# Local attention scores on both row halves of the array, two PSUM banks for them, and attention work at fixed slots

## The chip, the core and the metric

One core of a Trainium2 chip runs the whole program. Its engines are PE (TensorE, the matrix multiplier), DVE (VectorE), ACT (ScalarE) and POOL (GpSimd); SP issues the DMA transfers. Matmul results land in PSUM, which has eight banks of 512 fp32 per partition; DVE and ACT read PSUM, POOL does not. The metric is device time in microseconds (us), lower is better. Three runs of the kernel before took 862.6 to 864.3 us, median 864.2.

## What is computed

```python
scores = scale * np.matmul(q, k.transpose(0, 1, 3, 2))     # B=8, H=8, S=576, D=64
mask_local = (rel >= 0) & (rel < stride)                   # heads 0..3, stride 32
mask_strided = (rel >= 0) & (pos[None, :] % stride == pos[:, None] % stride)   # heads 4..7
attn = softmax(np.where(mask, scores, -1e9))
x = (attn @ v) as (4608, 512)                              # tokens by heads*dims
h = x @ w_in                                               # 512 -> 2048
out = (h * cos(h)) @ w_out                                 # 2048 -> 512
```

All data are fp32, and fp32-like precision is kept by splitting operands into a high and a low part.

## The kernel before

**Two stages.** The first stage (up to about 480 us) computes attention and `h`; the second (line L705) multiplies `h*cos(h)` with `w_out`. The change touches the first stage only.

**Slots.** In the first stage the hidden products of batch b are issued on PE in 56 slots per batch (`PER_BATCH`): about one product in each slot, six matmuls of 128x128 by 288 columns (L499 for batch 0, L528 later). Products write the banks `m` (three buffers), `n` and `o`. The attention of batch b+1 is put between the products of batch b, so that it is ready when batch b+1 begins. `in_turn` fixes PE's order to the order of the code; the other engines' order is made by a scheduler that lists instructions by their estimated readiness.

**Attention units.** A batch has four strided units and three local units. A unit is: loads of `qk` and `v`; scores on PE into a PSUM bank; softmax (DVE adds the mask, takes the maximum, subtracts, all from PSUM; ACT takes exp; DVE sums, adds an epsilon and inverts; POOL multiplies, line L284); a transpose (strided: PE, L383, then ACT copies to `pt`, L387; local: DVE, L322); products with `v` on PE (strided L396, local L331); copies out of PSUM (strided: ACT, L404 and L410; local: ACT L350 and DVE L351).

A fp32 matmul counts as two passes in the profile. A local unit has 24 score matmuls of a 64-row by 32-column tile of the array, 64 columns streamed (L314); its four heads use four of the eight such tiles: column quarter c, row half c mod 2. A strided unit has 10 or 12 score matmuls on two of the four 64x64 tiles (L366); a strided product uses the other two (L396). A burst is what is issued in one go: the products of an earlier unit with the scores of a new one. In strided bursts the two are interleaved matmul by matmul, in local bursts the products stand first and the scores behind.

**Where bursts stand.** Bursts are spread evenly by interpolation (`KNOTS`), 5.2 slots apart up to slot 48, then 8. A strided unit's transposes come 3 slots after the next burst; its products come in the burst of the strided unit after the next, so that two strided units are under way. A local unit is multiplied in the next local burst.

**PSUM banks of attention in these slots.** Scores of both kinds: `acc0` (zeroed once by one wide matmul, L262, and then always written with the flag that starts an accumulation). Strided transposes, and the local products of heads 2 and 3: `acc1`. Strided products, and the local products of heads 0 and 1: `acc2`. So a bank that scores leave late delays only the next scores, and a late copy out of `acc2` delays only the next products.

**Around the start of batch 1.** Between slots 47 and 57 of each batch the seven operands of the next batch are made: DVE subtracts (L465), ACT rounds to the high part (`x_hi`, L179), POOL takes the low part (`x_lo`, L180). In batch 0 and the first slots of batch 1 POOL also has the sums and low parts of `w_in` (L180, L206 to L212).

## Time and profile before

| | us |
|---|---|
| median of three runs (lowest, highest) | 864.2 (862.6, 864.3) |
| the profiled execution | 862.53 |
| its span, first to last instruction | 860.7 |
| PE busy | 849.2 (99%) |
| second stage (L705), from 480.4 us on | 376.8 of the chain |

The granted clock is 1.00 throughout. PE is the bound: time changes where PE's own work changes, or where PE waits. The trace is to be read for two things: how long PE is held by each kind of burst, and how late DVE, ACT and POOL hand back the banks and tiles that PE waits for. The rows are in the section below the next one.

### The profile page before, as it was taken

How to read it: one execution, taken by the hardware profiler on the slowest of the kernel's cores; microseconds unless marked ns; L12 is line 12 of the kernel's file. 1: busy time of each engine (PE TensorE's matmuls, PEld its weight loads, DVE VectorE, ACT ScalarE, POOL GpSimd, SP SyncE). 2: the span in 40 equal slices, each digit the busy share in tenths (PEclk: the TensorE clock that was granted, in tenths of full speed). 3: DMA queues.
4: the chain of work that ended last, by engine and by line, in shares of the span. 5: the costliest groups of instructions: out<-in, count | busy, mean ns of one | idle time of the engine just before them, and what ended most of it. 6: DMA issues, size and time to landing. Idle time of an engine off the chain costs nothing.

```text
span 860.7 us, 23160 instructions
## 1 busy us (share of the span) xinstructions
PE 849.2 (99%) x9147; PEld 792.2 (92%) x9147; DVE 569.3 (66%) x1087; ACT 529.1 (61%) x1031; POOL 540.1 (63%) x543
## 2 busy tenths in 40 slices
PE   9899999999999999999999999999999999999998
PEld 5799999999999999999999889999999999999996
DVE  5888766758667667686433667767777676767671
ACT  3766545545444454454457787777777777777772
POOL 2578984416216144162175489889888989898961
PEclk9999999999999999999999999999999999999999
DMA  9688444565667566765466844444444444444330
GB/s 335 207 272 298 140 161 167 177 211 196 240 214 240 195 226 227 233 218 201 152 198 210 283 123 135 123 126 132 124 124 130 126 123 126 132 125 130 118 129 28
DMA packets 91902, 151.82 MB, mean 176 GB/s; under 512 B 8465, under 2 KB 53009, under 8 KB 91793
## 3 DMA queue, kind: packets, MB, share of 16 engines
q1 hardware_dynamic: 91072, 150.11, 53.2%
q8 instruction: 72, 1.18, 0.6%
q14 instruction: 38, 0.30, 0.1%
q10 hardware_dynamic: 720, 0.23, 0.1%
HBM read 96.30 MB, written 54.00 MB: 175 GB/s over the span
## 4 chain that ended last, share of the span: by engine, by line
PE 89%; POOL 3%; DMA 3%; DVE 2%; ACT 2%; issue 1%; SPq 0%; DVEq 0%; ACTq 0%; POOLq 0%
PE q L705 44%; PE m L528 19%; PE n L528 10%; PE o L528 5%; PE m L499 4%; PE acc L331 2%; PE acc L396 2%; PE acc L314 2%; POOL x_lo L180 2%; DMA h_all<-h 1%; PE acc L383 1%; PE acc L366 1%; DMA v<-in_qkl 1%; DMA v<-in_qkvs 0%; PE m L314 0%
## 5 line engine op out<-in xcount | busy, mean ns | idle before, releaser
L705 PE MATMUL q<-w,g_hi 128*128 128x512 f32 (+1 forms) x1000 | 200.3, 339 | 0.0
L705 PEld LDWEIGHTS q<-w,g_hi 128*128 128x128 f32 x1000 | 161.1, 190 | 21.2
L180 POOL TENSOR_TENSOR g_lo<-g,g_hi 128x896 fp32r<-128x896 f32 x78 | 165.6, 2137 | 7.5 <-ACT g_hi L179 6.7
L705 PE MATMUL q<-w,g_lo 128*128 128x512 f32 (+1 forms) x500 | 111.7, 339 | 0.0
L528 PE MATMUL m<-x_hi,v 128*128 128x288 f32 x448 | 110.0, 300 | 1.2 <-ACT m L536 1.2
L528 PE MATMUL m<-x_hi,w 128*128 128x288 f32 x448 | 109.2, 298 | 0.8 <-DVE h L546 0.8
L651 DVE SCALAR_TENSOR_TENSOR r<-wave,h_in 128x512 f32<-128x512 int32 x144 | 96.1, 685 | 15.4 <-ACT wave L650 13.9
L653 ACT ACTIVATE wave<-r,quarter 128x512 f32<-128x512 f32 x144 | 98.7, 690 | 6.2 <-DVE r L651 5.9
L179 ACT CAST g_hi<-g 128x896 fp32r<-128x896 f32 x78 | 73.7, 944 | 40.4 <-POOL g L674 28.0
L705 PEld LDWEIGHTS q<-w,g_lo 128*128 128x128 f32 x500 | 83.5, 190 | 10.2
L650 ACT ACTIVATE wave<-h_in 128x512 int32<-128x512 f32 x144 | 83.8, 593 | 7.7 <-DVE g_lo L180 7.5
L705 PE MATMUL q<-v,g_hi 128*128 128x256 f32 x624 | 87.6, 283 | 0.0
L705 PEld LDWEIGHTS q<-v,g_hi 128*128 128x128 f32 x624 | 80.5, 192 | 0.0
L528 PEld LDWEIGHTS m<-x_hi,v 128*128 128x128 f32 x448 | 78.0, 188 | 2.5 <-ACT m L536 1.7
L528 PEld LDWEIGHTS m<-x_hi,w 128*128 128x128 f32 x448 | 78.0, 188 | 2.0 <-DVE h L546 1.3
L284 POOL TENSOR_TENSOR pn_s<-e_sb,z 128x324 f32<-128x324 f32 x28 | 21.0, 750 | 93.2 <-DVE z L282 62.6
L180 DVE TENSOR_TENSOR g_lo<-wave,g_hi 128x512 fp32r<-128x512 f32 x54 | 37.2, 689 | 55.5 <-PE q L705 55.3
L536 ACT COPY m<-m 128x288 f32<-128x288 f32 x112 | 44.6, 398 | 45.6 <-PE m L528 39.3
L284 POOL TENSOR_TENSOR e_sb<-e_sb,z 128x384 f32<-128x384 f32 x24 | 20.3, 845 | 76.6 <-DVE z L282 72.7
L528 PE MATMUL m<-x_lo,w 128*128 128x288 f32 x224 | 66.1, 295 | 0.0
L528 PE MATMUL m<-x_lo,v 128*128 128x288 f32 x224 | 66.1, 295 | 0.0
L671 POOL TENSOR_TENSOR g<-g 128x256 f32<-128x256 f32 x78 | 57.8, 741 | 6.1
(137 smaller groups left out, 2054.5 us busy)
## 6 DMA issues: line engine op xcount, KB each, us to landing
h_all<-h SPq DMA_DIRECT2D x128, 288.0 KB, 2.8
h_in<-h_all SPq DMA_DIRECT2D x144, 256.0 KB, 2.8
qk<-in_qkvs SPq DMA_DIRECT2D x28, 324.0 KB, 4.2
out<-o SPq DMA_DIRECT2D x35, 256.0 KB, 3.1
qk<-in_qkl SPq DMA_DIRECT2D x21, 416.0 KB, 4.2
raw<-in_w_in SPq DMA_DIRECT2D x16, 512.0 KB, 5.4
raw<-in_w_out SPq DMA_DIRECT2D x16, 512.0 KB, 4.9
v<-in_vl SPq DMA_DIRECT2D x24, 224.0 KB, 3.8
```

The source lines that it names most:

```text
L179: with_product(cast(out=hi, in_=x))
L180: return rest.tensor_tensor(out=lo, in0=x, in1=hi.bitcast(F32), op=ALU.subtract)
L284: nc.gpsimd.tensor_tensor(out=pn, in0=e, in1=z[:, :n].unsqueeze(2).broadcast_to([P, n, w]), op=ALU.mult)
L314: self.scored = self.pe(nc.tensor.matmul(s_ps[quarter_of(c), t * KW:(t + 1) * KW], q_t[half(j), p, QB * t:QB * (t + 1)], k_t[half(j), p, Q ...
L499: in_turn(nc.tensor.matmul(self.banks[i, j], a[:, c * P:(c + 1) * P], y[:, c], start=k == 0 and m == 0, stop=k == 1 and m == len(ops) - 1, ...
L528: in_turn(nc.tensor.matmul(bank, a[:, c * P:(c + 1) * P], y[:, c], start=first and i == 0, stop=i == len(ops) - 1, skip_group_check=True,))
L536: nc.scalar.copy(out=t, in_=self.bank[name[0]])
L650: with_product(nc.scalar.activation(out=k, in_=h, func=AF.Copy, scale=1.0 / (2.0 * math.pi), bias=0.25))
L651: nc.vector.scalar_tensor_tensor(out=r, in0=k, scalar=-2.0 * math.pi, in1=h, op0=ALU.mult, op1=ALU.add)
L653: sin = nc.scalar.activation(out=wave, in_=r, func=AF.Sin, bias=quarter)
L671: by_gpsimd(pool.tensor_tensor(out=g[:, 5:7], in0=g[:, 0:5:4], in1=g[:, 1:2].broadcast_to([P, 2, P]), op=ALU.subtract))
L705: in_turn(nc.tensor.matmul(at, a, w, start=first, stop=True, skip_group_check=True))
```

## The change

1. **Local scores on eight tiles.** From batch 1 on, a local unit's six query blocks are split in two halves ("sides") of three. Side 1 has the row halves of its heads exchanged (host layout: `turned`, `twice`), so that the four heads of both sides fill all eight 64x32 tiles. Each side writes a PSUM bank of its own: one tile `wide` of two banks holds the scores. The 24 matmuls are the same; they are issued four of side 0, four of side 1, in turn. DVE's three operations read both banks in one instruction. The load of `qk` grows from 832 to 896 columns.
2. **Banks.** `wide` takes the places of `acc0` and `acc1`. Strided scores use its first bank. Strided transposes, strided products and the local products of heads 0 and 1 share the one bank `acc`; the local products of heads 2 and 3 go to `o`, the bank of the hidden product in slots 2, 9, 16 and so on. The scratch of the conversion of `w_in` changes between `n` and `o` accordingly. `pt` has one buffer.
3. **Fixed slots.** From slot 85 on strided bursts stand 14 slots apart (slots 1, 15, 29, 43 of a batch), local ones in slots 5, 19 and 33; before that two lists give them. Strided transposes come 9 slots after the scores (11 later on), and the products in the next strided burst: one strided unit is under way and not two.

```diff
+SPLIT = LU // 2
+QKT = QKL + 2 * QB
...
-LOCAL = (1, 3, 5)
-TURNED = 3
-KNOTS = ((UNITS, 1), (2 * UNITS + 2, PER_BATCH - 8), (B * UNITS + 2, (B - 1) * PER_BATCH - 8))
+AT_ONCE = 2
+LOCAL_AT = (33, 61, 75)
+STRIDED_AT = (43, 57, 71, 85)
+FIRST_LOCAL = (5, 19, 33, 47, 61, 75)
+FIRST_STRIDED = (1, 13, 25, 37, 48, 60, 73, 86)
+TURNED = (9, 11)
...
+            self.wide = ps.tile([P, AT_ONCE, 512], F32, name="wide")
...
-                self.scored = self.pe(nc.tensor.matmul(
-                    s_ps[quarter_of(c), t * KW:(t + 1) * KW], q_t[half(j), p, QB * t:QB * (t + 1)],
-                    k_t[half(j), p, QB * t:QB * t + KW], start=b > 0, stop=True, skip_group_check=True,
-                ))
+                side, n = divmod(t, SPLIT) if b else (0, t)
+                at = QB * (t + side)
+                to = (sides[side] if b else s_ps)[quarter_of(c), n * KW:(n + 1) * KW]
+                self.scored = self.pe(nc.tensor.matmul(
+                    to, q_t[half(j ^ side), p, QB * t:QB * (t + 1)], k_t[half(j ^ side), p, at:at + KW],
+                    start=b > 0, stop=True, skip_group_check=True,
+                ))
...
-        att.banks(False, (acc[0],), (acc[1],), (acc[2],), (acc[1],))
+        att.banks(False, (), (acc[2],), (acc[2],), (o,))
...
+        for kind, (starts, regular) in enumerate(((FIRST_STRIDED, STRIDED_AT), (FIRST_LOCAL, LOCAL_AT))):
+            row = [unit for of_batch in units for unit in of_batch[kind]]
+            starts = [*starts, *(PER_BATCH * b + at for b in range(1, B) for at in regular)][:len(row) + 1]
+            for at, done, unit in zip(starts, [None, *row], [*row, None]):
+                bursts.setdefault(at, []).append((done, unit))
+                if unit and kind == 0:
+                    turns.setdefault(at + TURNED[at > PER_BATCH + 56], []).append(unit)
```

**How it moves instructions, three places.** The first is PE before the start of batch 1. In the kernel before, the fourth local burst stands in slot 41 and the next strided one in slot 48, seven products later (`acc0_656` is the bank of all scores, L499 a hidden product):

```order
L331 MATMUL acc2_1527<-pt_l_1251,v_1183 64x32 x2
L331 MATMUL acc1_1528<-pt_l_1251,v_1183 64x32 x2
L314 MATMUL acc0_656<-qk_1529 32x64 x24
L499 MATMUL m_1519<-x_hi_128,w_1303 128x288
L499 MATMUL m_1519<-x_lo_129,w_1303 128x288
L499 MATMUL m_1519<-x_hi_128,w_1303 128x288 x2
L499 MATMUL m_1519<-x_lo_129,w_1303 128x288
L499 MATMUL m_1519<-x_hi_128,w_1303 128x288
```

In the changed kernel the fourth local burst is in slot 47 and the strided one in slot 48, with one hidden product (L525) between them (L335 are local scores, L423 and L390 the strided products and scores):

```order
L353 MATMUL acc_1544<-pt_l_1335,v_1267 64x32 x2
L353 MATMUL o_1545<-pt_l_1335,v_1267 64x32 x2
L335 MATMUL wide_124<-qk_1546 32x64 x24
L525 MATMUL m_1537<-x_hi_131,w_1354 128x288
L525 MATMUL m_1537<-x_lo_132,w_1354 128x288
L525 MATMUL m_1537<-x_hi_131,w_1354 128x288 x2
L525 MATMUL m_1537<-x_lo_132,w_1354 128x288
L525 MATMUL m_1537<-x_hi_131,w_1354 128x288
L423 MATMUL acc_1631<-pt_1524,v_1391 64x54
L390 MATMUL wide_124<-qk_1632 54x54
```

The scores of both bursts go to `wide`, and what stood seven products apart now stands one apart.

The second place is POOL for the strided unit scored in slot 48: its multiplication is the last row. Before:

```order
L284 TENSOR_TENSOR e_sb_1587<-e_sb_1587,z_1593 128x384 [waits DVE_49,Activation_49]
L180 TENSOR_TENSOR x_lo_1657<-x1_975,x_hi_1656 128x576 [waits Activation_49]
L180 TENSOR_TENSOR w_887<-v_795,w_887 128x256 [waits Activation_49]
L212 TENSOR_TENSOR sums_1638<-v_795,sums_1638 128x256 [waits Pool_49]
L180 TENSOR_TENSOR x_lo_1712<-t_1660,x_hi_1711 128x576 [waits Activation_49]
L180 TENSOR_TENSOR x_lo_1731<-x0_1090,x_hi_1730 128x576 [waits Activation_49]
L180 TENSOR_TENSOR v_1759<-sums_1638,v_1759 128x768 [waits Activation_49]
L180 TENSOR_TENSOR x_lo_1763<-t_1734,x_hi_1762 128x576 [waits Activation_49]
L180 TENSOR_TENSOR x_lo_1784<-x0_1090,x_hi_1783 128x576 [waits Activation_49]
L284 TENSOR_TENSOR pn_s1_121<-e_sb_1697,z_1703 128x6x54 [waits DVE_49,PE_49]
```

Changed (`e_sb_1604` is the local unit of slot 47, `pn_s0_120` the strided one of slot 48; PE transposes it in slot 57, before it was slot 59):

```order
L185 TENSOR_TENSOR x_lo_1618<-x1_1029,x_hi_1617 128x576 [waits Activation_49]
L185 TENSOR_TENSOR w_896<-v_789,w_896 128x256 [waits PE_49,Activation_49]
L292 TENSOR_TENSOR e_sb_1604<-e_sb_1604,z_1610 128x384 [waits DVE_49]
L185 TENSOR_TENSOR x_lo_1675<-t_1621,x_hi_1674 128x576 [waits Activation_49]
L217 TENSOR_TENSOR sums_1526<-v_789,sums_1526 128x256 [waits Pool_49]
L185 TENSOR_TENSOR x_lo_1694<-x0_883,x_hi_1693 128x576 [waits Activation_49]
L185 TENSOR_TENSOR v_1722<-sums_1526,v_1722 128x768 [waits Activation_49]
L185 TENSOR_TENSOR x_lo_1726<-t_1697,x_hi_1725 128x576 [waits Activation_49]
L292 TENSOR_TENSOR pn_s0_120<-e_sb_1660,z_1666 128x6x54 [waits DVE_49,PE_49,Activation_49]
```

The local unit's multiplication now stands between the operands' low parts, one `x_lo` fewer is ahead of the strided one, and its transposes come two slots sooner and without a local burst between.

The third place is ACT behind the next strided burst (slot 63 before, slot 60 now). Before, the copy out of the strided products is that of `acc2_1950`:

```order
L179 CAST w_1050<-v_907 128x256 [waits Pool_49]
L536 COPY m1_1937<-m_1930 128x288 [waits PE_49,Activation_49]
L179 CAST v_1939<-sums_1879 128x768 [waits Activation_49,Pool_49]
L404 COPY x0_1979<-acc2_1950 128x6x18x3 [waits PE_49]
L536 COPY n1_2008<-n_2001 128x288 [waits PE_49]
L278 ACTIVATE e_sb_1981<-e_sb_1981 128x324 [waits DVE_49]
```

Changed, `acc_1814` holds the strided products of slot 60, and `acc_1854` the local products of slot 61, in the same bank:

```order
L414 COPY pt_1779<-acc_1775 128x324 [waits PE_49]
L562 COPY n1_1804<-n_1797 128x288 [waits PE_49]
L562 COPY m2_1812<-m_1763 128x288 [waits PE_49]
L184 CAST w_1053<-v_916 128x256 [waits Pool_49]
L431 COPY x0_1841<-acc_1814 128x6x18x3 [waits PE_49,Activation_49]
L286 ACTIVATE e_sb_1843<-e_sb_1843 128x324 [waits DVE_49]
L372 COPY x1_1908<-acc_1854 128x192 [waits PE_49]
```

The copy stands behind a rounding of weights that waits for POOL in both kernels; in the changed one the next burst, a slot later on PE, needs the bank that this copy empties.

## Rows read from the trace of the kernel before

**Rows 1.** The page, parts 1 and 4: busy time; chain by engine.

```profile
PE 849.2 (99%) x9147; PEld 792.2 (92%) x9147; DVE 569.3 (66%) x1087; ACT 529.1 (61%) x1031; POOL 540.1 (63%) x543
...
PE 89%; POOL 3%; DMA 3%; DVE 2%; ACT 2%; issue 1%; SPq 0%; DVEq 0%; ACTq 0%; POOLq 0%
```

**Rows 2.** Stretches: length, busy us of PE, PEld, DVE, ACT, POOL, clock, DMA.

```profile
92.00:116.00 24.00, 22.80 (x382) 21.50 (x381) 15.23 (x31) 11.68 (x26) 22.82 (x22) 1.00 0.40 134
...
480.00:861.00 381.00, 377.17 (x2439) 345.59 (x2438) 257.70 (x420) 279.25 (x450) 313.75 (x330) 1.00 0.42 128
```

**Rows 3.** Waits of PE: for whom, us in total, times, longest.

```profile
PE m L528 <- ACT m L536: 1.2, 2, 0.7
...
PE acc L383 <- POOL pn_s L284: 0.7, 1, 0.7
```

**Rows 4.** PE in time: start us, us, operation; a local burst.

```profile
113.68 1.02 PE L331 MATMUL acc<-pt_l,v 32*64 32x32 f32 x56
114.62 0.88 PE L314 MATMUL acc<-qk 64*32 64x64 f32 x48
115.43 0.40 PE L528 MATMUL n<-x_hi,w 128*128 128x288 f32 x1
```

**Rows 5.** PE in time, prologue: shorter runs of local scores.

```profile
17.85 0.41 PE L314 MATMUL m<-v 64*32 64x64 f32 x12
...
19.40 0.75 PE L314 MATMUL m<-v 64*32 64x64 f32 x36
```

**Rows 6.** PE in time: strided scores alone, and strided products alone.

```profile
33.75 0.81 PE L366 MATMUL acc<-qk 64*54 64x54 f32 x24
...
412.04 0.91 PE L396 MATMUL acc<-pt,v 54*64 54x54 f32 x24
```

**Rows 7.** PE in time, slot 48: interleaved strided burst, first row, next product.

```profile
89.45 0.26 PE L396 MATMUL acc<-pt,v 54*64 54x54 f32 x1
...
90.19 0.40 PE L499 MATMUL m<-x_hi,w 128*128 128x288 f32 x1
```

**Rows 8.** PE in time, prologue: ten wide matmuls like the one that zeroes.

```profile
24.34 2.33 PE L800 MATMUL m<-warm 128*128 128x512 bf16 x10
```

**Rows 9.** Slot 41 in time: end of local scores on PE, then DVE.

```profile
82.79 0.61 PE L314 MATMUL acc<-qk 64*32 64x64 f32 x30
...
83.15 1.36 DVE L465 TENSOR_TENSOR t<-x 128x576 f32<-128x576 f32 x1
84.43 0.55 DVE L275 TENSOR_TENSOR acc<-acc,ml 128x384 f32<-128x384 f32 x1
...
85.61 0.56 DVE L277 TENSOR_TENSOR e_sb<-acc,mx 128x384 f32<-128x384 f32 x1
```

**Rows 10.** POOL in time, slots 47 to 62, with what ended an idle time.

```profile
88.50 0.84 POOL L284 TENSOR_TENSOR e_sb<-e_sb,z 128x384 f32<-128x384 f32 x1
89.28 1.43 POOL L180 TENSOR_TENSOR x_lo<-x,x_hi 128x576 fp32r<-128x576 f32 x1
...
91.36 1.27 POOL L212 TENSOR_TENSOR sums<-v,sums 128x256 f32<-128x256 f32 x1
...
95.39 2.37 POOL L180 TENSOR_TENSOR v<-sums,v 128x768 fp32r<-128x768 f32 x1
...
100.45 1.26 POOL L284 TENSOR_TENSOR pn_s<-e_sb,z 128x324 f32<-128x324 f32 x1
...
103.05 0.74 POOL L206 TENSOR_TENSOR sums<-v 128x256 f32<-128x256 f32 x1
```

**Rows 11.** ACT in time behind the strided burst of slot 63.

```profile
105.90 0.41 ACT L179 CAST w<-v 128x256 fp32r<-128x256 f32 x1 [1.77 <-POOL v L207]
...
108.72 0.48 ACT L404 COPY x<-acc 128x324 f32<-128x324 f32 x1
```

**Rows 12.** DVE in time at a later batch's edge: strided scores read late.

```profile
258.89 0.50 DVE L275 TENSOR_TENSOR acc<-acc,ms 128x324 f32<-128x324 f32 x1 [0.26 <-PE acc L366]
...
263.27 0.48 DVE L277 TENSOR_TENSOR e_sb<-acc,mx 128x324 f32<-128x324 f32 x1
```

More of the change, by code (lines that the diff above doesn't have):

```diff
@@ L248, in bank @@
             pool, name = next(kind)
-            return pool.tile([P, 512], F32, name=name)
+            return self.wide[:, name] if pool is None else pool.tile([P, 512], F32, name=name)
         def score_bank(self, b, mask):
@@ L259, in score_bank @@
                 return bank
-            if self.kept is None:
-                self.kept = self.bank(self.scores)
-                in_turn(nc.tensor.matmul(
-                    self.kept, warm, warm.unsqueeze(1).broadcast_to([P, 4, P]), start=True, stop=True
-                ))
-            return self.kept
-        def softmax(self, b, s, mask, n, w, pn=None):
-            e = self.wk.tile([P, SC], F32, name="e_sb", bufs=3)[:, :n * w].rearrange("p (t w) -> p t w", w=w)
-            mx = self.sm.tile([P, SU], F32, name="mx")
-            most = mx[:, :n].unsqueeze(2).broadcast_to([P, n, w])
-            if b == 0:
-                nc.vector.tensor_reduce(out=mx[:, :n], in_=s, op=ALU.max, axis=AX.X)
-                nc.vector.tensor_tensor(out=e, in0=s, in1=most, op=ALU.subtract)
-            else:
+            if self.blank:
+                self.blank = False
+                for i in range(AT_ONCE):
+                    in_turn(nc.tensor.matmul(
+                        self.wide[:, i], warm, warm.unsqueeze(1).broadcast_to([P, 4, P]), start=True, stop=True
+                    ))
@@ new lines, in score_bank, with like @@
+            return self.wide
+        def softmax(self, b, s, mask, n, w, pn=None):
+            def like(t):
+                return t if len(s.shape) == 3 else t.rearrange("p (g t) -> p g t", g=s.shape[1])
+            flat = self.wk.tile([P, SC], F32, name="e_sb", bufs=3)[:, :n * w].rearrange("p (t w) -> p t w", w=w)
+            e = flat if len(s.shape) == 3 else flat.rearrange("p (g t) w -> p g t w", g=s.shape[1])
+            mx = like(self.sm.tile([P, SU], F32, name="mx")[:, :n])
+            most = mx.unsqueeze(len(s.shape) - 1).broadcast_to(list(s.shape))
+            if b:
@@ L275, in softmax @@
                 nc.vector.tensor_tensor(out=s, in0=s, in1=mask, op=ALU.add)
-                nc.vector.tensor_reduce(out=mx[:, :n], in_=s, op=ALU.max, axis=AX.X)
-                nc.vector.tensor_tensor(out=e, in0=s, in1=most, op=ALU.subtract)
-            exps.append(nc.scalar.activation(out=e, in_=e, func=AF.Exp, scale=0.125))
+            nc.vector.tensor_reduce(out=mx, in_=s, op=ALU.max, axis=AX.X)
+            nc.vector.tensor_tensor(out=e, in0=s, in1=most, op=ALU.subtract)
+            exps.append(nc.scalar.activation(out=flat, in_=flat, func=AF.Exp, scale=0.125))
@@ L418, in units @@
                 return [self.strided(b, *at) for at in s] + [self.local(b, u) for u in l]
-            s, l = iter(s), iter(l)
-            return [self.local(b, next(l)) if n in LOCAL else self.strided(b, *next(s)) for n in range(UNITS)]
+            return [self.strided(b, *at) for at in s], [self.local(b, u) for u in l]
     def stage(unit):
@@ L790, in attention_cos_ffn @@
         m, n, o = ((pools[name], name) for name in "mno")
-        acc = [(ps, f"acc{i}") for i in range(3)]
+        acc = [(None, 0), (None, 1), (ps, "acc")]
         att.banks(True, (m,), (o,), (acc[1], acc[2]), (acc[0], o))
         operands[0] = FirstOperands()
-        units = [unit for b in range(B) for unit in att.units(b)]
-        spare = ps.tile([P, 512], F32, name="acc0")
+        units = att.units(0)
+        spare = att.wide[:, 0]
         def keep_busy(bank, n, after):
@@ L823, in attention_cos_ffn @@
             list(input_weights(cv, 1, i))
[L824 to L827 removed]
+        att.banks(False, (), (acc[2],), (acc[2],), (o,))
         bursts, turns = {}, {}
[L829 to L840 removed]
+        units = [att.units(b) for b in range(1, B)]
+        for kind, (starts, regular) in enumerate(((FIRST_STRIDED, STRIDED_AT), (FIRST_LOCAL, LOCAL_AT))):
[5 more added lines that the diff above has]
+                    turns.setdefault(at + TURNED[at > PER_BATCH + 56], []).append(unit)
         plan = {}
@@ L965, in _layouts @@
     ql = np.stack([qp[..., LQ * u:LQ * (u + 1)] for u in range(NLU)], axis=1).reshape(B, NLU, P, 2 * LQ)
-    kl = np.stack([kp[..., LQ * u:LQ * u + LK] for u in range(NLU)], axis=1).reshape(B, NLU, P, 2 * LK)
+    kl = np.stack([kp[..., LQ * u:LQ * u + LK] for u in range(NLU)], axis=1)
+    edge = SPLIT * QB
+    ends = kl[..., edge:]
+    ql = ql.reshape(B, NLU, P, 2, LQ)
+    turned = np.concatenate([ql[..., edge:][:, :, half] for half in (slice(D, P), slice(0, D))], axis=2)
+    ql[1:, ..., edge:] = turned[1:]
+    ends = np.concatenate([ends[:, :, half] for half in (slice(D, P), slice(0, D))], axis=2)
+    twice = np.concatenate([kl[..., :edge + STRIDE], ends], axis=-1).reshape(B, NLU, P, 2 * (LK + QB))
+    kl = np.concatenate([kl.reshape(B, NLU, P, 2 * LK), np.zeros((B, NLU, P, 2 * QB), np.float32)], axis=-1)
+    kl[1:] = twice[1:]
+    ql = ql.reshape(B, NLU, P, 2 * LQ)
     vl = np.stack([vp[:, :, LQ * u:LQ * u + LK] for u in range(NLU)], axis=1)
```

52 lines of the change are left out of this document (27 added, 25 removed).

## The prediction

> **What bounds the kernel now.** I read the page's busy times first: PE is busy for 99% of the span, and the chain of work that ended last runs on PE for 89% [rows 1]. Then the two stages as stretches. In the second, PE is busy for 377.17 of 381.00 us [rows 2]; the change does not touch it, so I leave it as it is. In the first stage time changes by two things alone: what a burst costs on PE, and how long PE waits. So I read next what PE waits for; the two waits at the start of batch 1 that matter here are 0.7 us each, one for ACT's copy out of `m`, one for POOL's multiplication before a transpose [rows 3]. In the stretch around that place, 92 to 116 us, POOL is busy for 22.82 of 24.00 us, as much as PE [rows 2]: whatever the change makes PE wait for on POOL there has no slack to be caught up from. Last I read bursts on PE instruction by instruction, and the latencies of DVE, ACT and POOL behind them. A slot's hidden product is six matmuls of about 0.133 us, 0.80 us in all; I use that as the step between slots.
>
> **Eight tiles instead of four (the gain).** 24 score matmuls are 48 passes, and four tiles take four of them side by side, a round. The local scores take 0.88 us for 48 passes [rows 4], 0.75 us for 36 and 0.41 us for 12 [rows 5]. From 12 to 48 passes that is 0.47 us for 36, or 13.06 ns a pass and 52 ns a round of four; the rest is fixed. Does a second set of tiles really run beside the first? Strided scores alone on two tiles take 0.81 us for 24 passes [rows 6]; the interleaved strided burst puts 48 passes on four tiles, and goes from 89.45 us to the next product at 90.19 us [rows 7], so 0.74 us. Twice the passes on twice the tiles take no longer. With eight tiles the 48 passes are 6 rounds and not 12: 6 times 52 ns = 0.31 us less for one unit. Three units in each of the batches 1 to 7 are 21: 6.5 us, less the little that the alternation costs, so I take **-6.4 us**. The bounds are 0 (tiles of different banks do not run side by side) and -6.5.
>
> The Trainium skill, page "TensorEngine Tiling (Array Packing)", section "PSUM Bottleneck", says that tiling makes TensorE faster but not the evacuation of PSUM, so that the copy out may become the bound. The rows of DVE in the next part but one agree in kind: its three readings of the scores last as long as before while the scores get shorter. By that rule alone the gain is kept where the bank is wanted late, and is lost where it is wanted a slot later.
>
> **One strided burst fewer; one zeroing more.** With one strided unit under way and not two, there are 29 strided bursts and not 30. Before, the last one is products alone, 0.91 us from 412.04 us on [rows 6]; such a burst goes away, and the last scores now have their products in the burst behind: **-0.9 us**, between 0 and -1. `wide` needs one more wide matmul to zero it: ten of that shape take 2.33 us [rows 8], so **+0.2 us**.
>
> **The start of batch 1 (the cost).** I count from the end of the local scores of slot 47, as t = 0. Three waits of PE follow from each other.
>
> First, the scores of slot 48, due at t = 0.9 (one product). They write the first bank of `wide`, which DVE empties with mask, maximum and subtraction. In slot 41 of before, where nothing wants the bank, the scores end at 83.40 us and the subtraction at 85.61 + 0.56 = 86.17 us, after a subtraction for an operand (1.36 us) that stood ahead [rows 9]: 2.77 us. In the changed kernel up to 0.5 us of other work may stand between. PE waits 1.9 to 2.4 us; I take 2.2.
>
> Second, the transposes of that unit in slot 57. POOL has the local unit's multiplication at 88.50 us in rows of before, 5.1 us after the scores' end (83.40). Behind it the changed order has low parts (1.43 us), sums of weights (0.74 to 1.27), two more low parts (one of them the wide `v`, up to 2.37), one more `x_lo`, and then the strided multiplication (up to 1.26) [rows 10]. From 0.84 for the first on, these sum to 8.5 to 10, so the multiplication is done at t = 13.6 to 15.1. PE wants it after the strided burst (from 3.1 on, 0.9 long) and nine products (7.2): at about t = 11.2. The wait is 2.4 to 3.9; I take 3.0. In before the same wait is 0.7 [rows 3]. POOL is full here, so nothing shortens this by itself.
>
> Third, the products of the local unit in slot 61. They need bank `acc`, which ACT empties of the strided products of slot 60; that copy (0.48 us) stands behind a rounding of weights which in before waits 1.77 us for POOL already [rows 11]. After the strided multiplication POOL still has three `x_lo` (4.3 us) and two steps of the weights (0.74 each, [rows 10]) to do; with the rounding (0.41) and the copy (0.48) that makes 6.6 to 6.9 us. PE wants the bank after the transposes (0.3), three products (2.4) and the burst of slot 60 (0.8), 3.6 us after the multiplication. It waits about 3.0 us. All that is queued behind it on PE waits too, and on ACT the copies behind the rounding.
>
> Two smaller ones: bursts four slots apart, slots 1 to 5 and 33 to 37, allow 3.2 us where the bank is handed back after about 3.6 us: 0.4 us each. Sum of the boundary: 2.2 + 3.0 + 3.0 + 0.8 = **+9.0 us**, between 4 (the waits overlap, POOL's order gets ahead) and 11. In return the two waits of before, 0.7 + 0.7 [rows 3], go: **-1.4**.
>
> **The later batches.** Strided and local bursts stand 10 or more slots apart, 8 us or longer, except from slot 1 to slot 5: four products and the local products, 4.15 us. At such an edge in before the strided scores end at about 258.9 us, where DVE's mask starts after 0.26 us of waiting for them, and the subtraction ends at 263.27 + 0.48 = 263.75 [rows 12], 4.9 us later, since DVE also prepares the next operands. Units of other batches take 1.7 us. I take two of the six edges over by 0.6: **+1.2 us**, between 0 and 6 (each by 1).
>
> **The sum.** Against the profiled execution: 862.5 - 6.4 - 0.9 + 0.2 + 9.0 - 1.4 + 1.2 = 864.2 us. That execution lies at the low end of the runs shown (862.6 to 864.3), 1.7 us below their median; I put my median between, at **865.0**.
>
> **The rivals.**
>
> *The boundary costs little.* For it: waits on PE delay the work that DVE and POOL have to keep pace with, and a scheduler's order of POOL that looks late here could be early if operands come sooner. Against it: POOL's 22.82 of 24 us [rows 2]. With the wait for the bank alone (2.2), or half of the three, the boundary is 2 to 5 us instead of 9: **858 to 861**, clearly faster.
>
> *The pair of slots 1 and 5 stalls at every edge.* This is the other side. Place: the local scores of slot 5 of batches 2 to 7, and their products, which need `acc` after ACT's copy of the strided products. Price: the 4.9 us of [rows 12] against 4.15, and a copy that stands behind other ACT work, together about 1 us at each of six edges instead of 1.2 in all: +5, so **870**. It decides from where DVE is later than 4.15 us at most of the edges.
>
> *Eight tiles do not run at once.* Then the change does not do what it says: the scores of both sides take turns, and the 6.4 us do not come: **871.4**. The 48 passes of a burst start within 0.81 us, from 114.62 to 115.43 [rows 4], 17 ns each, and [rows 7] shows four tiles at the time of two; both speak against it, though 13 ns a pass may already be near what the sequencer can issue. With eight tiles it would have to be about 7 to 10.
>
> The Trainium skill, page "TensorE: Matmul & The Clock Gate", section "Wait — 56ns, not 53.3ns?", gives a floor for start-to-start of about 25 ns however small the matmul. By that rule 48 passes would take 1.2 us on any number of tiles, and this rival would hold. The trace disagrees for tiled bursts: 17 ns each in [rows 4]. So I give it little.
>
> **How the numbers follow.** The forecast, the boundary paying back the gain (861 to 868), gets 0.44; the cheap boundary 0.35; the stalls at every edge 0.12; no gain from eight tiles 0.08; 0.01 is left. A measurement of this kernel can tell about 0.2%, 1.7 us, from no change, so "same" is 862.5 to 865.9. Of the forecast 0.05 lies below that, 0.23 in it and 0.16 above. Of the cheap boundary 0.31 is faster and 0.04 the same. The other two are slower. So faster is 0.36, same 0.27, slower 0.37. The range, 857.5 to 870.0, takes in the forecast and nearly all of the cheap boundary and cuts off half of the stalls at every edge, and the last rival. Cases of both signs hold most of the chance; the forecast's own range is 861 to 868.
>
> **What the profile would show.** Right: local scores of about 0.57 us instead of 0.88 from batch 1 on; 29 strided bursts; PE's waits led by the strided scores waiting for DVE's subtraction, the transposes for POOL's multiplication and the local products for ACT's copy, two or three us each, all between 85 and 115 us; the second stage as long as now. Wrong: local bursts as long as before; or POOL's multiplication early, with no wait at slot 57; or waits of PE spread over the edges of all batches, which would be the second rival.

## The result and the profile after

The changed kernel takes 871.6 us (median of four runs, 870.4 to 872.0) against 863.4 us for the kernel before on the same chip: 1.0093 times as long, 95% interval 1.0075 to 1.0112. It is slower by 8 us, 1.6 us above the upper end of the predicted range.

The page of the kernel after, part 1 (busy time) and part 4 (chain by engine), to be read beside [rows 1]:

```profile
PE 852.0 (98%) x9148; PEld 793.3 (91%) x9148; DVE 560.8 (64%) x1087; ACT 529.9 (61%) x1031; POOL 537.8 (62%) x543
...
PE 89%; DVE 3%; POOL 2%; ACT 2%; DMA 2%; issue 1%; SPq 0%; DVEq 0%; POOLq 0%; ACTq 0%
```

PE is still the bound, with nearly the same busy time. The span grew from 860.7 to 869.5 us. The second stage did not change: the last hidden product starts at 479.34 us before and 488.17 after, and from there to the end it is 381.4 us in both. All of the loss is in the first stage.

Stretches of the kernel after (length, busy us of PE, PEld, DVE, ACT, POOL, granted clock, DMA); [rows 2] has the second of them for before:

```profile
20.00:40.00 20.00, 16.98 (x279) 12.91 (x278) 13.98 (x32) 13.53 (x33) 10.51 (x9) 0.83 0.54 179
...
92.00:116.00 24.00, 18.20 (x271) 16.91 (x272) 15.27 (x31) 10.93 (x25) 20.51 (x19) 0.87 0.37 119
```

In both stretches the granted clock, 1.00 in the kernel before, is lower, and at the start of batch 1 PE works 18.20 us where it worked 22.80. What PE waits for there (us in total, times, longest), to be held against [rows 3]:

```profile
PE acc L353 <- ACT x L431: 3.0, 1, 3.0
PE wide L390 <- DVE e_sb L285: 1.4, 1, 1.4
PE m L525 <- ACT h L534: 1.3, 1, 1.3
PE m L554 <- DVE h L532: 0.7, 1, 0.7
PE acc L407 <- POOL pn_s L292: 0.4, 1, 0.4
```

The local burst, as in [rows 4], in time on PE:

```profile
128.00 0.72 PE L335 MATMUL wide<-qk 64*32 64x64 f32 x48
128.65 0.40 PE L554 MATMUL n<-x_hi,v 128*128 128x288 f32 x1
```

The scores now take 0.65 us to the next product, where it was 0.81. That is a gain of 0.15 us, and half of what was forecast.

**Where the 8.8 us come from.** That is the difference of the two profiled executions (871.32 and 862.53 us). Counting hidden products (six matmuls each) on PE's time line gives their starts. Between two of them stands 0.80 us of work, the burst between them, and whatever PE waited.

| | before | after | |
|---|---|---|---|
| product 3 (first scores of batch 1 done) | 34.5 | 37.4 | +2.9: prologue |
| waits and slow work at products 39 to 87 | 1.6 | 10.9 | +9.3: start of batch 1 |
| local burst with products, typical of 20 | 1.84 | 1.69 | -3.0 in all |
| strided bursts | 30 | 29 | -0.9 |
| waits behind product 100 | 2.7 | 2.9 | +0.2 |
| last product | 479.3 | 488.2 | +8.8 (0.3 not placed) |

### The profile page after: what moved, and what is told of

The parts are those of the page before. It is cut to its first block, busy times and chain, and to the rows that moved or that the text cites. A ratio compares the mean times of both kernels' runs of the same rounds, so it can differ in the third digit from the quotient of the medians.

```text
span 869.5 us, 23157 instructions
## 1 busy us (share of the span) xinstructions
PE 852.0 (98%) x9148; PEld 793.3 (91%) x9148; DVE 560.8 (64%) x1087; ACT 529.9 (61%) x1031; POOL 537.8 (62%) x543
## 4 chain that ended last, share of the span: by engine, by line
PE 89%; DVE 3%; POOL 2%; ACT 2%; DMA 2%; issue 1%; SPq 0%; DVEq 0%; POOLq 0%; ACTq 0%
PE q L731 43%; PE m L554 19%; PE n L554 10%; PE o L554 5%; PE m L525 5%; PE acc L353 2%; PE acc L423 2%; PE wide L335 1%; POOL x_lo L185 1%; PE acc L407 1%; DMA h_all<-h 1%; PE wide L390 1%; DMA v<-in_qkl 1%; DMA v<-in_qkvs 1%; PE o L353 0%
## 5 line engine op out<-in xcount | busy, mean ns | idle before, releaser
L554 PE MATMUL m<-x_hi,v 128*128 128x288 f32 x448 | 108.3, 296 | 0.0
L184 ACT CAST g_hi<-g 128x896 fp32r<-128x896 f32 x78 | 73.5, 942 | 40.8 <-POOL g L700 28.1
L695 DVE TENSOR_TENSOR g<-wave,h_in 128x512 f32<-128x512 f32 x78 | 52.8, 683 | 13.0 <-ACT wave L679 13.0
```

What stands on the lines that cost most here:

```text
L184: with_product(cast(out=hi, in_=x))
L554: in_turn(nc.tensor.matmul(bank, a[:, c * P:(c + 1) * P], y[:, c], start=first and i == 0, stop=i == len(ops) - 1, skip_group_check=True,))
L695: nc.vector.tensor_tensor(out=g[:, :4].rearrange("p n t -> p (n t)"), in0=wave, in1=h, op=ALU.mult)
```

## Experiments

Times of the fifteen kernels are compared with runs of the kernel before on the same chip, which stood at 863.4 to 864.2 us. The changed kernel itself was timed in the first set alone (871.6 us), so differences to it go across sets. "Local bursts" are read as the start of the product behind less that of the product ahead less 0.80 us. All are edits of the changed kernel, where nothing else is said.

### Local bursts moved away from the strided ones

```diff
-FIRST_LOCAL = (5, 19, 33, 47, 61, 75)
+FIRST_LOCAL = (5, 18, 30, 42, 66, 78)
```

> The changed kernel with the local bursts of slots 5 to 75 moved to 5, 18, 30, 42, 66 and 78, so that none stands within five slots of a strided burst at the start of batch 1; everything else as changed. Theory (the neighbouring slots 47/48 and 60/61 make the waits, and the low clock that follows is a consequence of the waits): of the 8.8 us that PE loses between slots 55 and 71 of the trace, most goes; the wait of 3.0 us for ACT's copy before the local products and that of 1.4 us before the strided scores are gone, the granted clock in the stretch 92 to 116 us is 1.00 instead of 0.87, and the time is 5 to 8 us below the changed kernel, 864 to 867. Rival (POOL is full there, and whatever PE wants from it comes late in any slots): the waits turn up before the transposes of the strided unit of slot 48 instead, and the gain is under 2 us.

Measured: 870.3 us (1.0072, interval 1.0045 to 1.0100), 1.4 us below the changed kernel. The two waits named are gone and one stands in their place. PE's waits between 84 and 120 us:

```profile
PE acc L407 <- POOL pn_s L292: 3.6, 1, 3.6
```

The rival held: PE is earlier at slot 57 and finds POOL's multiplication not done. The clock fell after this wait too (0.89 in the stretch 90 to 120 us).

### Sides in sequence

```diff
-            turns = [n + SPLIT * side for n in range(SPLIT) for side in range(2)] if b else range(LU)
+            turns = range(LU)
```

> The changed kernel with the 24 local score matmuls issued side 0 first and then side 1, so that four tiles run at once and not eight; banks and slots as changed. Theory (alternating sides gains what the trace shows, 0.15 us a unit, since the last 16 of the 48 passes come at 16.5 ns each whatever the tiles): 21 times 0.15 = 3.2 us slower than the changed kernel. Rival (the gain is the 0.31 us of the prediction, and something else in the burst, such as the switch between the two kinds of tiles, got longer): the local scores take 0.88 us again and the burst as a whole is longer than before the change, 6 us slower. Second rival: no difference, the shorter burst of the changed kernel comes from the products.

Measured: 871.9 us, no difference to the changed kernel. Local bursts cost 1.74 instead of 1.69. The time is that of the second rival, but its reason is not the right one: the run with four tiles below shows that the shorter burst comes from the tiles. The order of the two sides is worth 0.05 us, and in the records passes 9 to 16 of a unit start eight in 57 ns, which one side on four tiles cannot do: it seems that matmuls of the second side start ahead of earlier ones that wait for their tile. So this run did not take the eight tiles away; a later one does.

### Work for PE in the wait before slot 61's products

```diff
+            if slot == 61:
+                for _ in range(10):
+                    in_turn(nc.tensor.matmul(
+                        att.wide[:, 1], warm, warm.unsqueeze(1).broadcast_to([P, 4, P]), start=True, stop=True
+                    ))
             for units_at in bursts.get(slot, ()):
```

> The changed kernel with ten wide matmuls of zeros (2.3 us at full clock) on PE just ahead of the local products of slot 61, into the second bank of the scores, which is free there: they add work into the 3 to 4 us in which PE has nothing. Theory (the granted clock fell to half from 110 to 117.5 us because PE had stood idle just before, and this costs about 3 us on top of the wait): the clock stays at 1.00 through 105 to 118 us, and the time is 2 to 3 us below the changed kernel, though work was added. Rival (the low clock comes from something else, or the work in that stretch is not bound by it): the time is the same or up to 2.3 us longer.

Stretches of the kernel after first, then of this one:

```profile
106.00:110.00 4.00, 1.24 (x47) 0.94 (x46) 1.50 (x3) 0.98 (x4) 4.00 (x5) 0.97 0.45 128
110.00:118.00 8.00, 7.71 (x123) 7.48 (x124) 4.83 (x13) 3.06 (x7) 6.01 (x8) 0.59 0.41 127
```

```profile
106.00:110.00 4.00, 2.42 (x55) 1.86 (x54) 1.51 (x4) 0.85 (x3) 4.00 (x5) 1.00 0.44 130
110.00:118.00 8.00, 8.00 (x141) 6.85 (x140) 4.82 (x13) 3.05 (x7) 6.00 (x8) 1.00 0.49 150
```

In the kernel after, PE is idle for most of 106 to 110 us, and in the 8 us behind it the clock is 0.59, most of the stretch at the lower of its two levels, 1.2 GHz. With the ten matmuls in the wait it stays at 1.00, and the local scores take 0.72 us and not 0.97:

```profile
110.29 0.37 PE L353 MATMUL acc<-pt_l,v 32*64 32x64 f32 x2 [3.05 <-ACT x L431]
...
111.72 0.97 PE L335 MATMUL wide<-qk 64*32 64x64 f32 x48
```

```profile
111.57 0.27 PE L353 MATMUL acc<-pt_l,v 32*64 32x64 f32 x2
...
112.40 0.72 PE L335 MATMUL wide<-qk 64*32 64x64 f32 x48
```

From the first of these local products to the start of product 72 it is 4.77 us (111.57 to 116.34) instead of 7.41 (110.29 to 117.70): the low clock costs 2.6 us there. The ten matmuls themselves held the local products back by 0.8 us, so from product 67 to product 72 1.9 us are gained (10.40 instead of 12.26), and product 136 starts 1.7 us sooner. But the time, 871.6 us, did not move. Between products 248 and 256 this kernel waits 1.8 us longer than the kernel after, on DVE's additions of `h`, which wait for stores. The size of the clock's share is shown at its place; that it would come out at the end is not.

### Prologue with tiles of one bank

```diff
-        acc = [(None, 0), (None, 1), (ps, "acc")]
+        acc = [(pe, "acc0"), (pe, "acc1"), (ps, "acc")]
...
+        early.close()
+        att.wide = pw.tile([P, AT_ONCE, 512], F32, name="wide")
```

> The changed kernel with two tiles of one bank each in the prologue, as before the change, and the tile of two banks only from the first slot on. The scheduler then puts PE's prologue in the order that it had before. Theory (the first hidden product starts 3.2 us later than before, at 32.9 instead of 29.6 us, because the tile of two banks makes the scheduler put the fourth unit of strided products behind the local products and a copy, and because the clock is at half from 25 to 31 us after PE's idle time): the first product starts at about 29.6 to 30 us and the time is 2.5 to 3.5 us below the changed kernel. Rival (the prologue is late for another reason, the larger loads or the other buffer of the transposed strided weights): first product still after 32 us, time as the changed kernel.

The first product starts at 30.06 us, 2.8 us earlier, so the tile of two banks did reorder the prologue: the scheduler held the last strided products of batch 0 back behind a copy out of the other bank of the same tile. In the kernel after, in time:

```profile
26.24 1.32 PE L423 MATMUL wide<-t,v 54*64 54x54 f32 x20 [0.60 <-DVE x_lo L367]
27.48 4.19 PE L825 MATMUL m<-warm 128*128 128x512 bf16 x10
```

and with tiles of one bank:

```profile
23.35 0.79 PE L422 MATMUL acc<-t,v 54*64 54x54 f32 x20
24.07 4.01 PE L828 MATMUL m<-warm 128*128 128x512 bf16 x10
```

The ten wide matmuls take 4.0 to 4.2 us at the lower clock in both, against 2.33 in [rows 8], so the edit did not bring the clock back. But the slow stretch is shorter (granted clock of 18 to 36 us 0.91 instead of 0.81), and the strided products in front take 0.79 us instead of 1.32: about half a microsecond of the 2.8 may be the clock's. In all eleven kernels with the one tile the first product starts at 32.1 to 36.4 us; in the three with two tiles, and in the kernel before and its variants, at 28.1 to 30.1.

Yet the time is 873.7 us, 2 us *longer*. What PE waits for between 84 and 120 us:

```profile
PE acc L406 <- POOL pn_s L291: 5.3, 1, 5.3
PE wide L389 <- DVE e_sb L284: 1.4, 1, 1.4
PE m L524 <- ACT h L533: 1.3, 1, 1.3
```

The earlier start turned into a longer wait for POOL (5.3 us instead of 0.4): product 136 starts at 181.94 us, as in the kernel after (181.96). But POOL did not stand still while PE came sooner. Its first low part is 3.3 us earlier too (86.85 us for 90.11), and its order is the same up to the `x_lo` that starts at 98.05 us, 101.31 in the kernel after. There the strided multiplication comes next; here the scheduler has put three operations ahead of it. POOL in time, with tiles of one bank:

```profile
98.05 1.41 POOL L185 TENSOR_TENSOR x_lo<-t,x_hi 128x576 fp32r<-128x576 f32 x1
99.41 1.40 POOL L185 TENSOR_TENSOR x_lo<-x,x_hi 128x576 fp32r<-128x576 f32 x1
100.77 1.24 POOL L211 TENSOR_TENSOR sums<-v 128x256 f32<-128x256 f32 x1
101.97 1.40 POOL L185 TENSOR_TENSOR x_lo<-t,x_hi 128x576 fp32r<-128x576 f32 x1
103.32 0.73 POOL L291 TENSOR_TENSOR pn_s<-e_sb,z 128x324 f32<-128x324 f32 x1
```

The three take 3.9 us (99.41 to 103.32), more than POOL was ahead. So the edit changed POOL's queue as well, and this run does not show what an earlier prologue is worth with POOL's order kept. The 2.0 us on top come behind product 136, in waits for `h` as above.

### Three low parts on DVE, in the kernel after and in the kernel before

```diff
-            split(self.raw[n] if x is None else x, hi, lo)
+            rest = nc.vector if self.first and n % 2 else nc.gpsimd
+            split(self.raw[n] if x is None else x, hi, lo, rest=rest)
```

> The changed kernel with three of the seven low parts of batch 1's operands (the second, fourth and sixth, 1.4 to 1.9 us each on POOL) taken by DVE instead of POOL; nothing else moved. The last runs showed the batch's start ending at about the same time, 110 to 112 us, whether PE came there 2.8 us earlier (prologue as before) or the local burst was moved away. Theory (POOL's chain of low parts, sums of weights and the two multiplications sets the end of that stretch, PE only fills it): 4.3 to 5 us less on POOL lets hidden product 72 start 3 to 5 us earlier than 117.7, and the time is 3 to 5 us below the changed kernel. Rival (ACT or DVE, which copy and round there, are just as late): DVE's work delays the hand-back of the score banks and the gain is under 1 us.

> The kernel before with the same three low parts of batch 1's operands on DVE. Theory: the kernel before loses only 1.6 us at this place (0.9 before the transposes, 0.7 for ACT's copy), so it gains at most that, 0 to 1.6 us. Rival (POOL costs both kernels alike): a gain of 3 us or more as in the changed kernel.

Measured: 872.3 us, no gain, and 864.4 us for the kernel before (1.0003, 0.9991 to 1.0015), as expected. Product 72 starts at 115.42 us, 2.3 us sooner than in the kernel after, but the wait changed its place. Between 84 and 120 us, first of PE's waits:

```profile
PE m L555 <- DVE h L533: 3.1, 1, 3.1
```

DVE took the low parts into a queue in which the copies of `h` out of `m` stand. The rival held as far as DVE goes.

### Later slots for all bursts at the start of batch 1

```diff
-FIRST_LOCAL = (5, 19, 33, 47, 61, 75)
-FIRST_STRIDED = (1, 13, 25, 37, 48, 60, 73, 86)
+FIRST_LOCAL = (5, 18, 30, 42, 68, 80)
+FIRST_STRIDED = (1, 13, 25, 37, 48, 64, 75, 87)
...
-                    turns.setdefault(at + TURNED[at > PER_BATCH + 56], []).append(unit)
+                    turns.setdefault(at + (13 if at == 48 else TURNED[at > PER_BATCH + 56]), []).append(unit)
```

> The changed kernel with local bursts at slots 5, 18, 30, 42, 68, 80 and strided ones at 1, 13, 25, 37, 48, 64, 75, 87; the transposes of the strided unit of slot 48 at slot 61. PE thus asks for POOL's multiplication about 4 us later than in the first of these runs, and for the bank behind ACT's rounding at slot 68. Theory (slots ask too early of a full POOL): the wait before the transposes shrinks from 4.3 us to about 1, no wait before the local products, and 4 to 6 us less than the changed kernel, 866 to 868. Rival (whatever the slots, some other engine holds PE up to 110 us): within 1.5 us of the first run's 870.3.

Measured: 864.1 us, 7.5 us below the kernel after and level with the kernel before (0.9997, 0.9986 to 1.0009). One wait is left between 84 and 120 us, and the stretch of 92 to 116 us looks like that of before:

```profile
PE acc L407 <- POOL pn_s L292: 1.3, 1, 1.3
```

```profile
92.00:116.00 24.00, 22.72 (x321) 21.80 (x312) 15.12 (x28) 11.44 (x27) 22.78 (x22) 1.00 0.41 138
```

Product 72 starts at 108.3 us and not 117.7, with one local burst (1.6 us) not yet done by then. Nothing but slots was changed, of bursts and of one unit's transposes: **the slots at the start of batch 1 are the cause of nearly the whole loss**, by way of the waits and the clock behind them.

### Which of the two pairs

As the last one, with `FIRST_LOCAL = (5, 19, 33, 47, 68, 80)`: the pair 47 and 48 stays.

> The changed kernel with the later slots of the 864.1 us run for the strided bursts and for the fifth and sixth local ones, but with the second to fourth local bursts left at 19, 33 and 47, so that the scores of slot 48 still follow those of slot 47 after one product. Theory (each pair costs its own waits): the 1.7 us before the scores of slot 48 stay, and the operands of batch 1 come later by the six slots between 42 and 47, so POOL and ACT are late behind them; 2 to 4 us above the 864.1, about 867. Rival (only the second pair, 60 and 61, and the early transposes cost): 864 to 865.5.

Measured: 869.0 us (1.0069, 1.0042 to 1.0095). The pair 47/48 and what comes of it (waits of 1.7, 1.4 and 0.9 us at products 55, 61 and 63) put product 72 at 111.04 us, 2.7 us behind the last run; of the rest of the 4.9 us, 1.5 stand in waits for `h` behind 120 us (3.2 us here, 1.7 in the last run with ACT's). Without the pair 60/61 and the early transposes, product 72 is 6.7 us ahead of the kernel after, 5.1 us once the local burst that it has not done yet (1.6) is taken off. Both pairs cost; the time of the whole, 2.6 us below the kernel after, shows less of it for the waits that come behind.

### Later sums of weights, in the kernel after and in the kernel before

```diff
-            in_steps(weight_sums(cv, f), *(16 + 10 * f + i for i in (0, 2, 5, 7)))
+            in_steps(weight_sums(cv, f), *(16 + 10 * f + (16 - 2 * f) * (f > 2) + i for i in (0, 2, 5, 7)))
```

> The changed kernel with the sums of the weights of the fourth block (four steps, 46 to 53) started ten slots later, and those of the blocks behind it by 8, 6, 4 and 2 slots: five POOL operations, 4.9 us, leave the stretch between the first operand of batch 1 and the strided multiplication, with no work given to DVE or ACT. Theory (POOL's queue sets when PE gets its transposes and, through ACT's rounding, the copied bank): the multiplication is done 3 to 5 us sooner than 103.4, hidden product 72 starts 3 us or more before 117.7, and the time is 3 to 5 us below the changed kernel's 871.6. Rival (after the run with three low parts on DVE, which gained nothing: what holds PE is not POOL's amount of work but the order of copies on ACT and DVE): product 72 within 1.5 us of 117.7 and the time within 1.5 us.

> The kernel before with the same later sums of weights. Theory: it loses 0.9 us before its transposes and 0.7 us to a copy there, so it gains 0 to 1.6 us. Rival: it gains as much as the changed kernel does by it, and then that run says nothing on the change.

Measured: 872.4 us, no gain, and 863.9 us for the kernel before (0.9992, 0.9974 to 1.0010). In its profiled execution the prologue was 3.5 us later than in that of the kernel after (clock 0.54 in 18 to 36 us); from product 54 to 72 it took 28.05 us instead of 30.49. So 2.4 us were gained at the place, and POOL's amount of work was no longer what was late; 2.2 of them are lost again behind product 72 (from there to the last product 372.6 us instead of 370.5). POOL in time:

```profile
93.91 1.58 POOL L185 TENSOR_TENSOR x_lo<-x,x_hi 128x576 fp32r<-128x576 f32 x1 [3.61 <-ACT x_hi L184]
97.83 0.83 POOL L292 TENSOR_TENSOR e_sb<-e_sb,z 128x384 f32<-128x384 f32 x1 [2.35 <-DVE z L290]
...
105.15 1.05 POOL L292 TENSOR_TENSOR pn_s<-e_sb,z 128x324 f32<-128x324 f32 x1 [1.31 <-DVE z L290]
```

Between its first low part and the strided multiplication POOL has three operations fewer than in the kernel after (0.74, 0.73 and 1.85 us, so 3.3 us and not the 4.9 that were expected). It stands idle for 7.3 us (3.61 + 2.35 + 1.31) and waits for ACT's rounding and DVE's sums. With the local products in slot 47, the first operand of batch 1 and two softmaxes come to DVE and ACT together. Relieving one engine moves the wait to the next; the slots load all three.

### What eight tiles are worth

Blocks in another order (`for n in (2, 0, 1)`), four tiles in the same two banks (`half(j)` for both sides), and the last eight matmuls twice (`for n in (0, 1, 2, 2)`):

> The changed kernel with the query blocks of each side in the order third, first, second. In the changed kernel the first 32 of a unit's 48 score passes start at 7 ns from each other (eight in 57 ns), then comes a gap of 84 ns, and the last 16 start at 16.5 ns. Theory (place in the burst decides: PE has only so many matmuls at hand): gap and slow passes stay behind pass 32, the local scores take 0.72 us as before. Rival (the third block's data or bank addresses are slow): the first 16 passes are slow, and the last 32 fast.

> The changed kernel with both sides of a local unit on the same row half, so that its scores use four tiles again, in two banks and in the changed order; the scores of side 1 are then wrong, and only the time is read. Theory (with four tiles the tiles set the pace, 57 ns for four passes): local bursts cost 1.83 us again instead of 1.69, as in the kernel before. Rival (the gain comes from the second bank or the order): they stay at 1.69 to 1.73.

> The changed kernel with the last eight score matmuls of every local unit issued twice (32 instead of 24, 64 passes; the same values are written again). Theory (behind the first 32 passes PE is fed one matmul in 33 ns, whatever the tiles): 16 passes more take 16 times 16.5 ns = 0.26 us, local bursts cost 1.95 us instead of 1.69. Rival (the tiles set the pace, eight passes in 57 ns): 0.11 us more, 1.80.

The four tiles, the kernel with other blocks first and the one with more scores, each with its scores and the product behind:

```profile
128.87 0.87 PE L335 MATMUL wide<-qk 64*32 64x64 f32 x48
129.68 0.40 PE L554 MATMUL n<-x_hi,v 128*128 128x288 f32 x1
```

```profile
126.76 0.72 PE L335 MATMUL wide<-qk 64*32 64x64 f32 x48
127.41 0.40 PE L554 MATMUL n<-x_hi,v 128*128 128x288 f32 x1
```

```profile
133.17 0.86 PE L335 MATMUL wide<-qk 64*32 64x64 f32 x64
133.95 0.40 PE L554 MATMUL n<-x_hi,v 128*128 128x288 f32 x1
```

With four tiles the burst costs 1.84 us as before the change, so the 0.15 us are the eight tiles', all of it. Single passes, from their records: on four tiles a round of four takes 55 to 57 ns throughout. On eight, a round of eight takes 55 to 57 ns (the first 80, on four tiles too), close to the 52 that were counted on, up to the 32nd pass. Then come 28 and 56 ns without a start, and the last 16 passes take about 190 ns, where two rounds of eight would be 114. With the other blocks first the same gap stands behind the same 32nd pass: the place decides, not the data. With 16 passes more the burst costs 1.82 and not 1.95, 0.13 us or 8.4 ns a pass: close to the pace of eight tiles (7.1), and my theory that PE is fed one matmul in 33 ns falls. What is lost is a gap of about 80 ns and a slow start behind it, once in a burst. What makes the gap after sixteen matmuls is open.

(The whole times of these three, single runs of 871.1, 874.7 and 880.9 us, are not read: other waits at the start of batch 1 moved with them.)

### The later slots with the rest mended

Later slots and the prologue's two tiles; then also the later sums:

> The changed kernel with the later slots of the 864.1 us run and the prologue's two tiles of one bank each, which let the first hidden product start 2.8 us earlier. Theory (POOL is behind at the batch's start, so PE's earlier arrival turns into a longer wait before the transposes of slot 61): the wait there grows from 1.6 to about 4 us, product 72 starts at about 108, and the time stays within 1 us of 864.1. Rival (with the later slots the prologue's gain is kept): 861 to 862.

> The three together: later slots, prologue with tiles of one bank, later sums of weights. Theory: neither POOL nor the slots nor the prologue hold PE then; the wait before the transposes of slot 61 is under 0.5 us, product 72 starts at 103 to 105 us, and what is left of the change, 0.15 us for each of 21 local units and 0.9 us for one strided burst fewer, shows: 860 to 862, 2 to 4 us below the kernel before. Rival (later waits for stores of h take it back, as in the run with the wide matmuls): 863 to 865.

Measured: 862.0 us (0.9983, 0.9968 to 0.9998), then 861.5 us (0.9976, 0.9962 to 0.9989). The first went against my theory, and the rival held (861 to 862): the wait before the transposes did not grow (1.3 us in both), and with the later slots, where POOL's order stayed as it was, part of the prologue's gain came through, 1.5 us at product 136 (172.9 for 174.4 us) and 2.2 us in the medians, whose intervals overlap. The second is what was forecast: between 84 and 120 us the wait for POOL is gone, and product 72 starts at 103.0 us, with the same bursts done as in the run at 108.3.

```profile
PE acc L422 <- ACT pt L413: 1.0, 1, 1.0
PE m L553 <- DVE h L571: 0.7, 1, 0.7
```

This version beats both kernels, by 0.24% and 1.2%. The later sums alone gave the kernel before nothing that can be told from no change.

## Why the prediction was wrong

**The start of batch 1: about right in sum.** I had forecast 9.0 us of waits. The starts of products show 10.9, of which 2.6 are the low clock, so 8.3. The first (scores of slot 48, 2.2) measured 1.7 between products (1.4 as the profile counts the wait). The second (transposes, 3.0) came as 0.7 at the transposes and 2.3 a few products ahead of them, where copies out of `m` were late: ACT's stood behind a rounding that waited for POOL's sums, DVE's behind the softmax of slot 48. ACT in time:

```profile
97.69 0.83 ACT L184 CAST v<-sums 128x768 fp32r<-128x768 f32 x1 [2.90 <-POOL sums L217]
...
99.01 0.39 ACT L534 COPY h<-m 128x288 f32<-128x288 f32 x1
```

So it was POOL's lateness again, by a way that I had not followed: every other thing that ACT copies behind a rounding. That the two parts add up to the 3.0 is luck. The third (local products of slot 61, 3.0) measured 3.05 on the row at 110.29 us above, with the releaser that was named: ACT, behind its rounding, behind POOL. The two smaller ones (0.8 together) did not come.

```profile
109.45 0.40 ACT L184 CAST w<-v 128x256 fp32r<-128x256 f32 x1 [2.62 <-POOL v L212]
109.76 0.47 ACT L431 COPY x<-acc 128x324 f32<-128x324 f32 x1
```

From the end of the local scores of slot 47 to the end of POOL's multiplication, in time:

```profile
89.04 0.72 PE L335 MATMUL wide<-qk 64*32 64x64 f32 x48
```

```profile
90.11 1.57 POOL L185 TENSOR_TENSOR x_lo<-x,x_hi 128x576 fp32r<-128x576 f32 x1 [1.31 <-ACT x_hi L184]
93.25 0.74 POOL L185 TENSOR_TENSOR w<-v,w 128x256 fp32r<-128x256 f32 x1 [1.56 <-ACT w L184]
94.31 1.25 POOL L292 TENSOR_TENSOR e_sb<-e_sb,z 128x384 f32<-128x384 f32 x1 [0.33 <-DVE z L290]
...
102.68 0.73 POOL L292 TENSOR_TENSOR pn_s<-e_sb,z 128x324 f32<-128x324 f32 x1
```

That is 13.65 us (89.76 to 103.41); the sum had 13.6 to 15.1 [rows 10]. But POOL was not full all the way: on these rows it waited 3.2 us for ACT and DVE (1.31 + 1.56 + 0.33), 2.2 of them within the 13.65. So "POOL is full" was half of the reason.

**Eight tiles: the term that was mis-sized.** Forecast -6.4 us, measured 0.15 for each of 21 units, -3.1. The step that failed is the rate: 13.06 ns a pass was taken from bursts on four tiles and carried on to eight as if rounds could not be interrupted. They can: after 32 passes stands a gap, and slow starts behind it; on four tiles no burst shows it. A row of 48 passes on eight tiles did not exist, and the bound of 0 was honest, but the value stood at the far end of it. The rival that eight tiles do not run at once is refuted: rounds of eight start 55 to 57 ns apart, where four tiles need that for four. (The burst that was read for four tiles in [rows 7] has 40 passes, 20 of each kind, and not 48. At equal numbers the reading stands: 0.81 us for 20 passes alone and 0.83 for 20 with 20, 0.93 for 24 alone and 0.93 for 24 with 24, between products.)

**The clock: left out.** "Time changes by two things alone" missed a third thing. The wait of 3.05 us, in a stretch of 4 us with 1.24 us of work on PE, was followed by work at half pace. That cost 2.6 us more, and the run that filled the wait did not pay them.

**The prologue: left out.** I costed the zeroing of a second bank and took the rest as it was. One tile of two banks is one thing to the scheduler, and it put batch 0's last strided products behind a copy. +2.9 us at product 3. Mended alone, the time did not fall, but POOL's order had changed with it; whether the kernel would hide this delay is not shown. With the later slots part of it came through.

**Later batches:** forecast +1.2, measured +0.2. The rival of stalls at every edge did not happen: in slot 5 of batches 2 to 7 one wait of 0.4 us is left, at product 123. The longest behind product 100, 1.3 and 0.8 us at products 255 and 249, stand in slots 25 and 19 of batch 4 and wait for DVE's additions of `h`. In sum the kernel before has nearly as much (2.7 us for 2.9). The rival of a cheap boundary did not happen either.

So the forecast had the place of the waits right; on the sign it was undecided (0.37 slower, 0.36 faster). From 864.2 us by my sum, the missing half of the gain (+3.4), the prologue (+2.9), the clock (+2.6), the waits at the start of batch 1 less those of before (-0.9), the later batches (-1.0) and 0.1 of small terms lead to 871.3 = 862.5 + 8.8. These are entries of an account; that they could be mended one by one is not shown, since an edit at one place changed the order of other engines' queues.

## What to carry to other kernels

A step that hands work to three engines in turn needs its slots set by the slowest way round, at the place where those engines are fullest; two bursts that share a bank, one product apart, cost more than the burst itself. Mend such a place by moving the demand: the slots gave 7.5 us, while taking work off POOL (twice, in two ways) gave nothing by itself. Two banks that are used apart should be two tiles for as long as they are, since a scheduler orders by tile; and a rate read from four units at once is a bound, not a value, for eight.

## What was not expected of the hardware

A long wait of PE was paid twice: behind about 4 us with little work (1.24 us from 106 to 110 us) the granted clock fell to 0.50 for some 6 us. In the prologue, too, it stood at the lower level, and ten wide matmuls took 4.19 us where they take 2.33. The shorter waits, 1.4 and 1.3 us from 90 to 100 us, left it at 1.00. Issued in sequence, the two sides lost only 0.05 us a unit, as if matmuls could start ahead of earlier ones whose tile is taken; that they do is read from start times alone. On eight tiles a burst runs 32 passes at 7 ns, then pauses for some 80 ns, in both orders of the data that were tried. And kernels that are level at product 136 differ by up to 2.6 us at the end (the kernel after and the one with the prologue's tiles of one bank), through waits on the stores of `h` whose times shift with everything ahead; a gain of under 2 us in the first half is not safe until it is seen at the end.
